# Attention and feed-forward on one core: outputs turned by DMA, loads on GpSimd, first values kept on chip, scores one block further ahead

## The chip, the core and the metric

The kernel runs on one core of a Trainium2 chip. The core has TensorE (PE in the profile, its weight loads PEld), VectorE (DVE), ScalarE (ACT), GpSimd (POOL) and SyncE (SP), each with its own instruction queue that runs in order, and 16 DMA engines that they share. The metric is the device time of one launch in microseconds (us); the median of several runs is compared.

## The reference

Two stages. Block-sparse attention over 4 batches, 8 heads, 768 positions, head size 64, in blocks of 32 positions (24 blocks): a query block sees its neighbours, the first and the last block, and three sampled blocks; the first and the last query block see everything. Then, on the 3072 tokens of 512 numbers, a bilinear feed-forward network (FFN) with 1536 hidden units.

```python
scores = (q @ k.T) / sqrt(64)
mask = |block_q - block_k| <= 1, or either is block 0 or 23, or block_k in sampled_blocks[block_q]
attn = softmax(where(mask, scores, -1e9))
x = (attn @ v), heads side by side          # 3072 x 512
out = ((x @ w_a) * (x @ w_b)) @ w_out       # 512 -> 1536 -> 512
```

## The kernel before

**Units and chunks.** A unit is one batch and one query block, 96 in all; 22 of each 24 are sparse (gathered keys and values), two are dense. Eight units make a chunk (256 tokens); there are twelve chunks, and the second chunk of the first batch is done first. For a unit, TensorE makes the scores of all eight heads (two quads of four heads, each head in 32 of 128 rows), VectorE finds the maximum, ScalarE takes the exponential, the weights are turned so that keys lie on partitions, and TensorE multiplies them with the values. The first batch works in float32 and turns with TensorE (`plain_turn`, L1039); the others split each float32 into two float16 halves (`in_parts`, L951 to L958) and turn by a DMA transpose on SyncE (L1135 sparse, L1239 dense).

**Gathers.** Each sparse unit needs its eight key blocks side by side (`gather_keys`, copies on GpSimd, L653 to L662) and its eight value blocks (`gather_after`, DMAs on SyncE, L714 to L719). Three block numbers are only known at run time: both gathers read them from a small table into registers first (L623, a TENSOR_LOAD). Both gathers have two buffers.

**Output of a pair of units.** `output` divides the sums by the denominators into `xs` (L1292, or L1294 to L1296), lets TensorE transpose it in two float32 matmuls into the sums' own PSUM bank (L1301), and writes the two float16 halves `xT` on ScalarE and VectorE (L1312, L1313).

**FFN.** For a chunk, 12 steps of 24 matmuls (L1350) give the two products of 128 hidden units each, which are multiplied into `g` (L1365, L1368). When all 12 are there, a scale is found, `g` is split (L1402, L1403), and 12 steps of six matmuls (L1432 to L1434) make the output, which ScalarE reads and stores (L1448, L1450). These matmuls fill TensorE between the units of later chunks.

**Weights.** The FFN's weights arrive as 36 tiles of 64-bit numbers (L842, DMAs issued by ScalarE) during the first batch; VectorE and ScalarE convert each tile (L865 to L871, L887 to L895).

**Order.** A planner in the kernel simulates the engines with a cost for each step and writes every engine's instructions out in the order that it finds; each engine then runs its list in order. `LAG` is one of its rules: from unit 24 on, a unit's scores come after the values of the unit three before it. DMAs of SyncE and ScalarE share eight semaphores in turn, so that each waits for the one eight before it to land.

## Time and profile before

| | |
|---|---|
| three runs | 824.20, 828.27, 829.44 us; median 828.27 |
| the profiled execution | 832.1 us, its span 830.3 us |
| TensorE busy | 757.6 us, 91% of the span |
| VectorE, ScalarE, GpSimd busy | 525.1, 485.3, 172.7 us |
| granted TensorE clock, mean | 0.971 of full speed |

The median is 3.8 us below the profiled execution. Busy time is the union of an engine's instructions. Queue instructions (DMA issues, register reads, semaphore waits) do not count as busy; the rows mark them with a q (SPq, ACTq, POOLq).

### The profile page before, as it was taken

The numbers are of one execution on the slowest core, as the hardware profiler recorded it, in microseconds if no ns is written. First come the engines' busy times: TensorE is split into PE (matmuls) and PEld (weight loads), VectorE is DVE, ScalarE is ACT, GpSimd is POOL, SyncE is SP. The second block draws the span as 40 slices with busy tenths as digits, with TensorE's granted clock in tenths as the row PEclk, the third lists the DMA queues.
The fourth block names the chain that finished last, engine by engine and source line by source line (L and its number), as shares of the span: only waits on it lengthen the run. The fifth ranks groups of instructions, "written<-read, shape, count | busy, mean of one in ns | idle before, by whom it ended". The sixth has DMA issues, their size and how long they took to land.

```text
span 830.3 us, 26115 instructions
## 1 busy us (share of the span) xinstructions
PE 757.6 (91%) x10128; PEld 533.0 (64%) x10128; DVE 525.1 (63%) x1495; ACT 485.3 (58%) x1189; POOL 172.7 (21%) x430
## 2 busy tenths in 40 slices
PE   3759699999997989899799999999999999999998
PEld 1426477764586468748558848848758668768853
DVE  3679998866746755686657676766566666532232
ACT  3456777886646554775645666766456655533333
POOL 4405321012123321130223221301123212000000
PEclk9859999999999899999999999999999999999999
DMA  7788877477577688869777779769776665440001
GB/s 226 224 280 252 240 198 213 147 206 176 135 149 144 139 213 148 178 167 185 175 162 137 151 181 228 174 162 188 148 151 148 128 124 128 111 116 2 1 1 52
DMA packets 171803, 130.50 MB, mean 157 GB/s; under 512 B 116894, under 2 KB 138527, under 8 KB 171679
## 3 DMA queue, kind: packets, MB, share of 16 engines
q1 hardware_dynamic: 156844, 86.29, 48.6%
q10 hardware_dynamic: 14832, 42.54, 17.0%
q8 instruction: 80, 1.31, 0.7%
q14 instruction: 47, 0.36, 0.1%
HBM read 86.31 MB, written 11.01 MB: 117 GB/s over the span
## 4 chain that ended last, share of the span: by engine, by line
PE 72%; DMA 10%; DVE 8%; ACT 5%; SPq 2%; issue 2%; ACTq 0%; POOL 0%; POOLq 0%; DVEq 0%
PE ab L1350 40%; PE o L1432 6%; PE o L1434 6%; PE o L1433 6%; PE av L991 5%; PE s L932 4%; DMA VG<-in_v_dram 3%; DMA keysT<-ks 2%; PE av L1301 2%; PE s L923 2%; DMA VG<-vd 2%; ACT gh L1402 1%; DVE gh L1403 1%; PE tp L1039 1%; DMA QZ<-in_q_dram 1%
## 5 line engine op out<-in xcount | busy, mean ns | idle before, releaser
L1350 PE MATMUL ab<-xT,wab 128*128 128x256 f16 x3456 | 396.0, 274 | 2.7 <-DVE g L1368 2.7
L1350 PEld LDWEIGHTS <-wab 128*128 128x128 f16 x3456 | 334.1, 98 | 58.1 <-issue 17.1
L1368 DVE TENSOR_TENSOR g<-g,ab 128x256 f32<-128x256 f32 x144 | 60.4, 419 | 145.8 <-ACT g L1365 141.9
L1365 ACT ACTIVATE g<-ab,f 128x256 f32<-128x256 f32 x144 | 67.9, 471 | 110.5 <-PE ab L1350 106.8
L1402 ACT ACTIVATE gh<-g,scale 128x256 f16<-128x256 f32 x144 | 70.5, 504 | 79.4 <-PE o L1434 74.0
L1403 DVE SCALAR_TENSOR_TENSOR gh<-g,scale,gh 128x256 f16<-128x256 f32 x144 | 68.8, 490 | 75.1 <-ACT gh L1402 73.9
L1432 PE MATMUL o<-wo,gh 128*128 128x512 f16 x288 | 110.4, 383 | 0.1
L1434 PE MATMUL o<-wo,gh 128*128 128x512 f16 x288 | 110.2, 383 | 0.0
L1433 PE MATMUL o<-wo,gh 128*128 128x512 f16 x288 | 110.2, 383 | 0.0
L653 POOL COPY KG<-keysT 128x384 int32<-128x384 int32 (+1 forms) x86 | 47.8, 556 | 278.8 <-PE s L932 237.8
L662 POOL COPY KG<-keysT 128x128 int32 (+1 forms) x264 | 92.6, 388 | 51.8 <-POOL KG L653 32.3
L1095 ACT ACTIVATE sm<-s,low,cq 128x256 f32<-128x256 f32 x132 | 73.7, 560 | 47.4 <-DVE low L1089 38.8
L991 PE MATMUL av<-VG,pt 128*32 128x128 f16 (+2 forms) x3584 | 68.4, 217 | 27.2 <-DMA VG<-in_v_dram 13.0
L421 POOL PARTITION_ALL_REDUCE power<-bound x58 | 22.7, 391 | 296.0 <-DVE bound L1382 126.9
L958 DVE SCALAR_TENSOR_TENSOR hl<-sm,hl 128x256 f16<-128x256 f32 (+1 forms) x156 | 69.6, 450 | 1.7
L1083 DVE TENSOR_REDUCE low<-s 128x2 f32<-128x512 f32 x88 | 60.2, 684 | 13.9 <-PE s L923 9.0
L991 PEld LDWEIGHTS <-pt 128*32 128x32 f16 x2688 | 33.0, 97 | 34.8 <-issue 22.5
L1434 PEld LDWEIGHTS <-gh 128*128 128x128 f16 x288 | 28.4, 99 | 34.6 <-issue 0.8
L1432 PEld LDWEIGHTS <-gh 128*128 128x128 f16 x288 | 28.2, 98 | 34.8 <-issue 4.3
L1433 PEld LDWEIGHTS <-gh 128*128 128x128 f16 x288 | 28.3, 98 | 28.6 <-issue 0.6
L1372 ACT ACTIVATE junk<-g 128x1024 f16<-128x1024 f32 x36 | 38.0, 1055 | 8.5 <-DVE g L1368 8.5
L954 DVE TENSOR_SCALAR hl<-sm 128x256 f16<-128x256 f32 (+1 forms) x125 | 39.3, 317 | 5.5 <-ACT sm L1095 5.2
(122 smaller groups left out, 876.0 us busy)
## 6 DMA issues: line engine op xcount, KB each, us to landing
VG<-vd SPq DMA_DIRECT2D x210, 64.0 KB, 2.2
VG<-vd SPq DMA_DIRECT2D x66, 192.0 KB, 3.2
VG<-vd SPq DMA_DIRECT2D x24, 384.0 KB, 3.8
out_dram<-ou ACTq DMA_DIRECT2D x24, 256.0 KB, 3.5
VG<-in_v_dram SPq DMA_DIRECT2D x74, 64.0 KB, 3.7
stage<-in_v_dram ACTq DMA_DIRECT2D x12, 384.0 KB, 6.7
q<-in_q_dram ACTq DMA_DIRECT2D x18, 256.0 KB, 4.6
vd<-vs SPq DMA_DIRECT2D x12, 384.0 KB, 4.2
```

The source lines that it names most:

```text
L662: nc.gpsimd.tensor_copy(to[:, :, (5 + r) * w : (6 + r) * w], of[:, :, bass.ds(at, w)])
L958: t = yield dve(221 + n * 1.03, lambda: nc.vector.scalar_tensor_tensor(lo, sm, over, hi, ALU.mult, ALU.subtract))
L991: mm(both[hs, :, i % 2, hq] if two else av[hs, i % 2, hq], pt[:, y, hs], of if two or b == 0 else of[:, 0], start=(i % 2 == 0 and hq == 0 ...
L1095: t = yield act(750, lambda hq=hq: nc.scalar.activation(sm[:, hq], ps[:, hq], AF.Exp, bias=low[:, at, hq, 0:1], scale=factor_of(b, cc, hq) ...
L1350: mm(ab[:, i, :], wab[:, f, i, part, kt, :], xc[:, kt, a, :], start=(i == 0 and kt == 0 and part + a == 0), stop=(kt == KT - 1 and a == 1) ...
L1365: yield act(460, lambda: nc.scalar.activation(g, ab[:, 0, :], AF.Copy, scale=f1[:, f : f + 1]))
L1368: t = yield dve(415, lambda: nc.vector.tensor_mul(g, g, ab[:, 1, :]))
L1402: yield act(400, lambda: nc.scalar.activation(gh[:, 0], g, AF.Copy, scale=s))
L1403: t = yield dve(480, lambda: nc.vector.scalar_tensor_tensor(gh[:, 1], g, s, gh[:, 0], ALU.mult, ALU.subtract))
L1432: mm(po, gh[:, 0, js], wo[:, f, 0], start=(f == 0), stop=False)
L1433: mm(po, gh[:, 0, js], wo[:, f, 1], start=False, stop=False)
L1434: mm(po, gh[:, 1, js], wo[:, f, 0], start=False, stop=(f == NF - 1))
```

## The change

Ten edits in one:

- `output`, batches 1 to 3: `xs` is split into two float16 halves `xo` (ScalarE, VectorE), one DMA transpose on SyncE writes them into `xT`, and the PSUM bank is given back once the sums are read. TensorE's transposes stay in batch 0 alone. The layout of `xT` changes for it: `[P, 4, 2, 2, KT, 32]` in place of `[P, KT, 2, 256]`, so an FFN matmul reads its 256 columns in eight runs of 32.
- All loads but those of the first batch's keys, queries, values and the tables, and the stores of the output, are issued by GpSimd instead of ScalarE (`pool_load`).
- SyncE reads the block numbers of up to four units with one TENSOR_LOAD (`starts_of`).
- The host lays the queries out twice (both partition halves), each load is twice as large, and the DMAs that copied one half to the other (`turn_queries`) are gone.
- The first batch's values are loaded once into three tiles in the buffers of `g` (`plain_values_in`). The first eight units (`NEAR`) take their three neighbouring blocks from there by copies on VectorE or ScalarE (`near_values`), and the dense unit (0, 0) reads them in place. Before, the values were loaded for their maximum into a part of the weights' tiles, which held back half of the weights (`parked`), and every gather read the DRAM.
- `LAG` is 4 instead of 3. `KS_BUFS` is 2 instead of 3; `xo` has two buffers.
- The planner's costs know GpSimd's DMAs, so all engines' lists are written anew.

```diff
-KS_BUFS = 3
+KS_BUFS = 2
+XO_BUFS = 2
+LATE_XO = 1000
+LATE_XT = 2500
...
+AT_ONCE = 4
+NEAR = 8
+LATE_X = 800
+LATE_X0 = 0
...
-LAG = 3
+LAG = 4
...
+
+
+def pool_load(moved, fn):
+
+    return [Way("POOL", 1000, fn, moved, 1000)]
...
     VG = [kvp.tile([P, 2, ROW], F16, name=f"VG{i}") for i in range(VG_BUFS)]
-    xT = [kvp.tile([P, KT, 2, CH], F16, name=f"xT{i}") for i in range(X_BUFS)]
+    xT = [kvp.tile([P, PER // 2, 2, 2, KT, BLK], F16, name=f"xT{i}") for i in range(X_BUFS)]
     plain_keys = keysT[0].rearrange("p h s -> p (h s)").bitcast(F32).rearrange(
...
     )
+    resident, resident_held = [], []
     plain_values = v[0].rearrange("g p x -> (g p x)").rearrange("(s x) -> s x", x=H * D)
...
-        yield load_way(1000, lambda: nc.scalar.dma_start(raw, k[b, g]))
+        yield pool_load(1000, lambda: nc.gpsimd.dma_start(raw, k[b, g]))
...
         k_ready[b].fire(end)
+    def plain_block(j):
+
+        t, at = divmod(j, P // BLK)
+        return resident[t // 2][at * BLK : (at + 1) * BLK, t % 2]
+
+    def plain_values_in(r):
+
+        resident_held.append((yield from take("g", G_BUFS)))
+        tt = work.tile([P, 2, H * D], F32, tag="g", name=f"vp{r}", bufs=G_BUFS)
+        resident.append(tt)
+        t = yield load_way(1300, lambda: nc.scalar.dma_start(
+            tt, plain_values.rearrange("(t p) x -> p t x", p=P)[:, 2 * r : 2 * r + 2]
+        ))
+        v_here.fire(t)
+        if r + 1 < NT // 2:
+            plan.start(plain_values_in(r + 1), R_V)
+        else:
+            plan.start(values(1, 0), order[1, 0] - LEAD_V)
+        done = yield from take("ks", KS_BUFS)
+        spare = work.tile([P, 2, H * D], F16, tag="ks", name=f"va{r}", bufs=KS_BUFS)
+        end = yield act(1060, lambda: nc.scalar.activation(
+            spare, tt, AF.Abs, accum_out=bound_v[:, r : r + 1]
+        ))
+        done.fire(end)
+        v_bound[0].fire(end)
+        if r == NT // 2 - 1:
+            plan.start(values_scale(0), order[0, 0] - LEAD_V)
+
     def values(b, g):
...
         raw, freed = yield from raw_tile(b, g, 1)
-        yield load_way(1000, lambda: nc.scalar.dma_start(raw, v[b, g]))
+        yield pool_load(1000, lambda: nc.gpsimd.dma_start(raw, v[b, g]))
         if g + 1 < NG:
-            plan.start(values(b, g + 1), order[b, 0] - LEAD_V if b else R_V)
-        elif b == 0:
-            plan.start(values(1, 0), order[1, 0] - LEAD_V)
+            plan.start(values(b, g + 1), order[b, 0] - LEAD_V)
         elif b + 1 < B:
...
         t = raw.rearrange("p (t x) -> p t x", t=NT)
-        done = yield from take("ks", KS_BUFS)
-        spare = work.tile([P, 2 * NT, P], F16, tag="ks", name=f"va{b}_{g}", bufs=KS_BUFS)
         end = yield act(1020, lambda: nc.scalar.activation(
-            spare[:, :NT], t, AF.Abs,
-            accum_out=bound_v[:, b * NG + g : b * NG + g + 1],
-        ))
-        done.fire(end)
+            junk.rearrange("p f c -> p (f c)")[:, : NT * P].rearrange("p (t x) -> p t x", t=NT),
+            t, AF.Abs, accum_out=bound_v[:, b * NG + g : b * NG + g + 1],
+        ))
         v_bound[b].fire(end)
...
             plan.start(values_scale(b), order[b, 0] - LEAD_V)
-        if b == 0:
-            freed.fire(end)
-            return
         yield v_scale[b]
...
         )[1]
+    def starts_of(b, i):
+
+        if (b, i) not in starts_kept:
+            c = i // PER
+            last = min(i + AT_ONCE, (c + 1) * PER, NB - 1)
+            got = nc.values_load_multi_w_load_instructions(
+                offs[0:1, i:last, :NR].rearrange("p a b -> p (a b)"),
+                engines=(mybir.EngineType.SP,), min_val=0, max_val=S - BLK,
+                skip_runtime_bounds_check_because="the table is clamped to these bounds",
+            )[1]
+            for x in range(i, last):
+                starts_kept[b, x] = got[(x - i) * NR : (x - i + 1) * NR]
+        return starts_kept.pop((b, i))
+
+    starts_kept = {}
     kg_holds, vg_holds = {}, {}
...
             yield from gather_after(n)
+    def near_values(b, i, to):
+        yield v_here
+
+        def copies(eng):
+            def fn():
+                for x in range(3):
+                    eng(to[x * BLK : (x + 1) * BLK, 0, :], plain_block(i - 1 + x))
+            return fn
+
+        t = yield [
+            Way("ACT", 1740, copies(nc.scalar.copy)),
+            Way("DVE", 1000, copies(nc.vector.tensor_copy)),
+        ]
+        vg_ready[b, i, 0].fire(t)
+
     def gather_after(n):
...
                 return
-            nc.sync.dma_start(to[0 : 3 * BLK, 0, :], of[(i - 1) * BLK : (i + 2) * BLK, :])
+            if not near:
+                nc.sync.dma_start(to[0 : 3 * BLK, 0, :], of[(i - 1) * BLK : (i + 2) * BLK, :])
             if first:
...
                 nc.sync.dma_start(to[0:BLK, 1, :], of[(NB - 1) * BLK :, :])
-            for r, at in enumerate(dynamic("SP", offs, i)):
+            for r, at in enumerate(starts_of(b, i)):
                 nc.sync.dma_start(
...
                 )
-        t = yield [Way("SP", 475 if dense else 2300 + 800 * first, copies, 1300, 1)]
+        near = order[b, i] < NEAR
+        if near:
+            plan.start(near_values(b, i, to), order[b, i] - LEAD_G)
+        t = yield [Way("SP", 475 if dense else 2300 - 700 * ((b, i) in starts_kept) - 400 * near + 800 * first, copies, 800 if near else 1300, 1)]
         vg_ready[b, i, x].fire(t + LATE_VG)
...
             t = work.tile([P, NG, CH], F32, tag="rq", name=f"q{cc}_{half}", bufs=1)
-            end = yield load_way(700, lambda t=t, half=half: nc.scalar.dma_start(
-                t[:D], q[b, c, :, half * NG : (half + 1) * NG]
+            end = yield pool_load(2000, lambda t=t, half=half: nc.gpsimd.dma_start(
+                t, q[b, c, :, half * NG : (half + 1) * NG]
             ))
...
         heads = slice(half * NG, (half + 1) * NG)
-        high, low_ = QT[cc][:D, 0, heads], QT[cc][:D, 1, heads]
+        high, low_ = QT[cc][:, 0, heads], QT[cc][:, 1, heads]
         yield act(1230, lambda: nc.scalar.activation(
-            high, t[:D], AF.Abs, accum_out=bound[:D, at : at + 1]
+            high, t, AF.Abs, accum_out=bound[:, at : at + 1]
         ))
...
         known.fire(end)
-        s = scale[:D, at : at + 1]
-        end = yield act(1120, lambda: nc.scalar.activation(high, t[:D], AF.Copy, scale=s))
-        plan.start(turn_queries(cc, half, 0), u0 - LEAD_Q, end)
+        s = scale[:, at : at + 1]
+        yield act(1120, lambda: nc.scalar.activation(high, t, AF.Copy, scale=s))
         end = yield dve(1250, lambda: nc.vector.scalar_tensor_tensor(
-            low_, t[:D], s, high, ALU.mult, ALU.subtract
+            low_, t, s, high, ALU.mult, ALU.subtract
         ))
         freed.fire(end)
-        plan.start(turn_queries(cc, half, 1), u0 - LEAD_Q, end)
+        q_ready[cc].fire(end)
     def next_queries(cc):
...
         )[half].bitcast(I32)[:, at * 2 * DM : (at + 1) * 2 * DM]
-        end = yield load_way(1350, lambda: nc.scalar.dma_start(
+        end = yield pool_load(1350, lambda: nc.gpsimd.dma_start(
             raw, (w_a, w_b, w_out)[i][f].bitcast(I32)
...
             yield act(470, lambda: nc.scalar.copy(xs, sums[:, 1]))
-            yield dve(418, lambda: nc.vector.tensor_add(xs, xs, sums[:, 0]))
+            t = yield dve(418, lambda: nc.vector.tensor_add(xs, xs, sums[:, 0]))
+            read.fire(t + LATE_AV)
             yield dve(430, lambda: nc.vector.tensor_mul(xs, xs, over))
-        ps = bank[:, 1].rearrange("p (g i x) -> p g i x", g=NG, i=2)
+            gone = yield from take("xo", XO_BUFS)
+            xo = work.tile([P, 2, 2, P], F16, tag="xo", name=f"xo{b}_{i}", bufs=XO_BUFS)
+            flat = xs.rearrange("p i a d -> p i (a d)")
+            yield act(400, lambda: nc.scalar.copy(xo[:, 0], flat))
+            t = yield dve(420, lambda: nc.vector.tensor_sub(xo[:, 1], flat, xo[:, 0]))
+            held.fire(t)
+            t = yield sp(900, 760, lambda: nc.sync.dma_start_transpose(
+                to.rearrange("p a x k q -> p (a x) (k q)"), xo.rearrange("p a i c -> p (a i c)")
+            ))
+            gone.fire(t + LATE_XO)
+            x_ready[cc].fire(t + LATE_XT)
+            x_ready[cc].fire(t + LATE_XT)
+            return
+        ps = bank[:, 1].rearrange("p (i c) -> p i c", i=2)
+        yield LATE_X if b else LATE_X0
         def turns_():
...
                 nc.tensor.transpose(
-                    ps[:, :, x], xs[:, x].rearrange("p a d -> p (a d)"), eye
+                    ps[:, x], xs[:, x].rearrange("p a d -> p (a d)"), eye
                 )
...
                                 mm(
-                                    ab[:, i, :], wab[:, f, i, part, kt, :], xc[:, kt, a, :],
+                                    ab[:, i, :].rearrange("p (j x q) -> p j x q", j=PER // 2, x=2),
+                                    wab[:, f, i, part, kt, :], xc[:, :, a, :, kt, :],
                                     start=(i == 0 and kt == 0 and part + a == 0),
...
-        t = yield load_way(728, lambda: nc.scalar.dma_start(rows, o))
+        t = yield pool_load(728, lambda: nc.gpsimd.dma_start(rows, o))
...
+        a = np.concatenate([a, a], axis=2)
```

Three places in the lists, before and now. First SyncE, in the third batch, between two units: `pt` is a unit's turned weights, `VG` the gathered values, `vd` the values in DRAM, `xo` and `xT` the output's halves before and after the turn. Before:

```order
L1135 DMA_TRANSPOSE pt_7845<-hl_7732 128x8x128
L714 DMA VG_85<-vd_80 96x1024
L623 TENSOR_LOAD offs
L719 ISA
L719 DMA VG_85<-vd_80 32x1024
```

and now:

```order
L1187 DMA_TRANSPOSE pt_7764<-hl_7685 128x8x128
L1368 DMA_TRANSPOSE xT_86<-xo_2_7836 128x4x128
L778 DMA VG_85<-vd_80 96x1024
L783 ISA
L783 DMA VG_85<-vd_80 32x1024
```

The register read is gone from most gathers (24 are left of 88), and every second unit a transpose of the outputs stands ahead of a gather.

Second TensorE, second batch, in the second products (`o`) of a chunk, between the steps of two hidden tiles `gh`. Before:

```order
L1434 LDWEIGHTS gh_0_4557
L1434 MATMUL o_1_4589<-wo,gh_0_4557 128x512
L1301 MATMUL av_6_4329<-eye,xs_6_4553 128x4x32 x2
L1432 LDWEIGHTS gh_1_4558
L1432 MATMUL o_0_4588<-wo,gh_1_4558 128x512
```

and now:

```order
L1514 LDWEIGHTS gh_0_4947
L1514 MATMUL o_1_4986<-wo,gh_0_4947 128x512
L1512 LDWEIGHTS gh_1_4948
L1512 MATMUL o_0_4985<-wo,gh_1_4948 128x512
L1513 LDWEIGHTS gh_1_4948
```

The pair of transposes between them is gone; of 48 such pairs in the list 12 are left, all in batch 0.

Third GpSimd, first batch, between the key gathers (`KG`) of two units. Before:

```order
L662 COPY KG_83<-keysT_76 128x4x32
L653 COPY KG_82<-keysT_76 128x4x96
L623 TENSOR_LOAD offs
L662 ISA
L662 COPY KG_82<-keysT_76 128x4x32
```

and now:

```order
L710 COPY KG_83<-keysT_76 128x4x32
L898 DMA stage<-in_moe_w_out_dram 128x1024
L701 COPY KG_82<-keysT_76 128x4x96
L656 TENSOR_LOAD offs
L710 ISA
L710 COPY KG_82<-keysT_76 128x4x32
```

A weight load now stands between two gathers on the same queue; the first two of the 36 stand ahead of the first gather.

## Rows read from the trace of the kernel before

**Rows 1.** The page: TensorE busy, and the granted clock, in 40 slices (tenths).

```profile
PE   3759699999997989899799999999999999999998
PEclk9859999999999899999999999999999999999999
```

**Rows 2.** Stretches: from:to, us, then each engine's busy us, clock, DMA share, GB/s.

```profile
0.00:60.00 60.00, 32.57 (x489) 17.29 (x489) 33.13 (x106) 29.24 (x80) 19.59 (x49) 0.82 0.79 237
60.00:140.00 80.00, 68.79 (x1036) 50.43 (x1037) 75.83 (x193) 57.05 (x153) 28.47 (x58) 0.92 0.77 228
220.00:760.00 540.00, 514.42 (x7347) 370.95 (x7346) 339.18 (x996) 311.79 (x771) 114.00 (x297) 0.99 0.72 154
260.00:280.00 20.00, 13.95 (x257) 8.20 (x248) 13.57 (x46) 14.00 (x35) 6.27 (x19) 0.83 0.75 146
300.00:320.00 20.00, 17.09 (x226) 13.97 (x225) 11.26 (x37) 11.30 (x26) 3.69 (x11) 0.91 0.82 193
400.00:420.00 20.00, 15.69 (x225) 7.88 (x222) 12.87 (x39) 10.76 (x26) 5.40 (x13) 0.91 0.67 156
```

**Rows 3.** Waits of TensorE, 0 to 60 us: us in total, times, longest.

```profile
PE s L1068 <- DVE mrows L497: 7.4, 1, 7.4
PE av L991 <- DMA VG<-in_v_dram: 6.6, 2, 3.9
PE s L923 <- DMA wab<-in_v_dram: 5.0, 1, 5.0
```

**Rows 4.** Waits of TensorE, 200 to 760 us.

```profile
PE av L1301 <- DVE xs L1296: 8.5, 8, 1.5
PE av L991 <- DMA VG<-vd: 5.9, 5, 2.9
PE av L991 <- DMA pt<-hl: 4.5, 1, 4.5
PE av L1301 <- ACT gh L1402: 4.5, 2, 4.2
```

**Rows 5.** Groups of TensorE by form, 220 to 830 us: busy, mean ns, idle before.

```profile
L991 PE MATMUL av<-VG,pt 128*32 128x128 f16 x1332 | 43.3, 224 | 10.5 <-DMA VG<-vd 5.9 <-DMA pt<-hl 4.5
L991 PE MATMUL av<-VG,pt 128*32 128x64 f16 x1332 | 40.0, 194 | 0.0
L1301 PE MATMUL av<-eye,xs 128*128 128x128 f32 x72 | 14.8, 287 | 13.7 <-DVE xs L1296 8.5 <-ACT gh L1402 4.5 <-DVE low L1089 0.4
```

**Rows 6.** Timeline of TensorE around 264 us: start, us, line, [idle before].

```profile
260.81 2.79 PE L1350 MATMUL ab<-xT,wab 128*128 128x256 f16 x24
...
264.51 0.43 PE L1301 MATMUL av<-eye,xs 128*128 128x128 f32 x2
269.45 0.83 PE L991 MATMUL av<-VG,pt 128*32 128x128 f16 x32 [4.51 <-DMA pt<-hl]
```

**Rows 7.** SyncE's queue by line: ns min/median/max, first to last start.

```profile
L1135 SPq DMA_TRANSPOSE pt<-hl x66: 1231/1274/2644, 231.2 to 716.6; - x66
L623 SPq TENSOR_LOAD <-offs x88: 662/684/1623, 13.7 to 714.3; - x88
L822 SPq DMA_DIRECT2D QT<-QT x36: 467/546/1271, 165.9 to 654.3; - x36
```

**Rows 8.** The page's DMA issues: KB each, median us to landing.

```profile
out_dram<-ou ACTq DMA_DIRECT2D x24, 256.0 KB, 3.5
pt<-hl SPq DMA_TRANSPOSE x90, 3.6
```

**Rows 9.** Groups by form, whole span, of the output's two halves.

```profile
L1312 ACT ACTIVATE xT<-av 128x256 f16<-128x256 f32 x36 | 13.5, 375 | 3.9 <-PE av L1301 3.9
L1313 DVE SCALAR_TENSOR_TENSOR xT<-av,xT 128x256 f16<-128x256 f32 x36 | 15.0, 418 | 1.9 <-ACT xT L1312 1.8
```

**Rows 10.** GpSimd's and ScalarE's queues by line: ns min/median/max, first to last start.

```profile
L623 POOLq TENSOR_LOAD <-offs x22: 724/728/955, 3.0 to 131.5; - x22
L842 ACTq DMA_DIRECT2D keysT<-in_moe_w_a_dram x8: 329/334/357, 31.5 to 145.7; - x8
```

More of the change, by code (lines that the diff above doesn't have):

```diff
@@ L182, in begin @@
         if way.moved:
-            at = max(at, self.dma - way.ahead, self.generator)
+            at = max(at, self.dma - way.ahead, self.generator if way.eng != "POOL" else 0.0)
             if len(self.landed) >= LANES:
@@ L193, in issue @@
             turn = way.eng == "SP" and way.ns != 650 and not way.extra
-            self.generator = at + (625 if turn else way.ns if way.extra else 455)
-            start = max(self.dma, at + (1275 if turn else 1100 if way.eng == "SP" else 1241))
+            if way.eng != "POOL":
+                self.generator = at + (625 if turn else way.ns if way.extra else 455)
+            begun = 1275 if turn else {"SP": 1100, "ACT": 1241, "POOL": 1900}[way.eng]
+            start = max(self.dma, at + begun)
             self.dma = start + way.moved
@@ L296 @@
     B, NCH, D, H, CH = q.shape
+    D //= 2
     NF, P, DM = w_a.shape
@@ L381 @@
     k_free = [Event(NB) for _ in range(B)]
-    v_bound = [Event(NG) for _ in range(B)]
+    v_bound = [Event(NG if b else NT // 2) for b in range(B)]
+    v_here = Event(NT // 2)
     v_scale = [Event() for _ in range(B)]
     v_stored = [Event(NG) for _ in range(B)]
-    q_ready = [Event(3 if cc < NCH else 5) for cc in range(NC)]
+    q_ready = [Event(3) for _ in range(NC)]
     tables = Event()
@@ L398 @@
         dense = i in (0, NB - 1)
+        if (b, i) == (0, 0):
+            continue
         vg_units += [(b, i, x) for x in range(2 * HQ if dense else 1)]
     vg_order = {u: m for m, u in enumerate(vg_units)}
-    vg_ready = {u: Event() for u in vg_units}
+    vg_ready = {u: Event(2 if order[u[:2]] < NEAR else 1) for u in vg_units}
     s_sent = {u: Event() for u in units}
@@ L508, in raw_tile @@
     def raw_tile(b, g, n):
-        if b == 0:
-            late = wab[:, NF // 2 :].rearrange("p f i a c x -> p (f i a c x)").bitcast(F32)
-            late = late.rearrange("p (g x) -> p g x", x=2 * NT * D)
-            return late[:, g], parked
         yield stage_freed
@@ L612, in values_scale @@
         yield dve(150, lambda: nc.vector.reduce_max(
-            bound[:, at : at + 1], bound_v[:, b * NG : (b + 1) * NG],
+            bound[:, at : at + 1], bound_v[:, b * NG : b * NG + (NG if b else NT // 2)],
             axis=mybir.AxisListType.X,
@@ L816, in plain_queries @@
         next_queries(cc)
-    def turn_queries(cc, half, a):
-        heads = slice(half * NG, (half + 1) * NG)
-        yield SPARE
-        end = yield sp(650, 400, lambda: nc.sync.dma_start(
-            QT[cc][D:, 1 - a, heads], QT[cc][:D, a, heads]
-        ))
-        q_ready[cc].fire(end)
     def weights(n):
@@ L1245, in all_values @@
     def all_values(b, i, hq, x, pt, kept):
-        m = vg_order[b, i, 2 * hq + x]
-        yield vg_ready[b, i, 2 * hq + x]
+        if (b, i) == (0, 0):
+            yield v_here
+        else:
+            m = vg_order[b, i, 2 * hq + x]
+            yield vg_ready[b, i, 2 * hq + x]
         if hq == 0 and x == 0:
@@ L1251, in all_values @@
             yield all_done[b, i, 2 * hq + x - 1]
-        if b == 0:
+        if (b, i) == (0, 0):
+            terms = [
+                (pt, (y,), resident[(3 * x + y) // 2][:, (3 * x + y) % 2, 4 * D * hq : 4 * D * (hq + 1)])
+                for y in range(3)
+            ]
+        elif b == 0:
             vg = plain_vg(m).rearrange("p a x -> p (a x)")
@@ L1261, in all_values @@
         kept.fire(t)
-        vg_free[m].fire(t)
+        if (b, i) != (0, 0):
+            vg_free[m].fire(t)
+        elif (hq, x) == (HQ - 1, 1):
+            for held in resident_held:
+                held.fire(t)
         all_done[b, i, 2 * hq + x].fire(t)
@@ L1309, in output @@
         s = scale[:, at_v : at_v + 1] if b == 0 else 1.0
-        of = ps.rearrange("p g i x -> p g (i x)")
-        hi, lo = to[:, :, 0], to[:, :, 1]
+        of = ps.rearrange("p i c -> p (i c)")
+        hi, lo = (to[:, a].rearrange("p x k q -> p (x k q)") for a in range(2))
         yield act(470, lambda: nc.scalar.activation(hi, of, AF.Copy, scale=s))
@@ L1461 @@
         plan.start(make_tables(), -40)
-        plan.start(values(0, 0), R_V)
+        plan.start(plain_values_in(0), R_V)
         plan.start(weights(0), R_L)
```

11 lines of the change are left out of this document (3 added, 8 removed).

## The prediction

> **What bounds the kernel now.** I read the page's slices first, then the busy times by stretch, then TensorE's waits, then the groups of the lines that the change touches. The slices [rows 1] show two regimes. In the first quarter TensorE's digits wander between 3 and 9 and its granted clock dips to 5, a slice in which it stood at its lower level, 1.2 of 2.4 GHz, for most of the time; from a quarter on they are 9 or close to it, with a few dents. The stretches [rows 2] put numbers to it. From 220 to 760 us TensorE is busy 514.4 of 540 us: its work is the bound there, and what leaves its list leaves the time. From 60 to 140 us VectorE is the fuller one, 75.8 of 80 us against TensorE's 68.8, while the weights are converted. Before 60 us nothing is full (TensorE 32.6, VectorE 33.1 of 60): the time goes by latencies, and the waits say which [rows 3]: 7.4 us for the mask at the start, 6.6 us for the gathered values of two units, 5.0 us for the first loads. After 200 us TensorE's waits are of two sorts [rows 4]: for `xs` ahead of its transposes (8.5 us; another 4.5 us ahead of the same transposes is put down to ScalarE's `gh`), and for a unit's gathered values or turned weights (5.9 and 4.5 us).
>
> **The change, part by part.** The sum is made against the profiled execution, 832.1 us.
>
> *Transposes of the output.* In batches 1 to 3, 72 of them go, 14.8 us of TensorE's busy time [rows 5]. They lie in the stretch where TensorE is the bound: 14.8 us gained.
>
> *The wait before them.* The same row shows 13.7 us of idle TensorE ahead of those matmuls. As TensorE runs its list in order, everything behind stood still for a result that only the next chunk needs. Now the list goes on; some of what comes next will not be ready either. Bounds 0 and 13.7; I take 11, nearer the upper end, since FFN matmuls mostly come next.
>
> *What replaces them.* ScalarE and VectorE lose 375 and 418 ns for each of 36 pairs and gain a copy and a subtraction of the same size [rows 9], so nothing. SyncE gains 36 transposes; an issue of the twice as large one takes 1.27 us [rows 7], so at most 46 us in 540. It loses three quarters of the register reads, 64 of 88 at 0.68 us, 44 us, and 36 copies of queries at 0.55 us, 20 us [rows 7]. Behind a transpose that waits for `xo` stand the next unit's value gathers. They have the fourth block of lead to hide in. `xT` is ready later than before by some 4 us: a landing takes 3.6 us behind the issue's start [rows 8], plus queueing, in place of a 0.43 us pair of transposes. If the cover of other matmuls is gone that delays the first product of a chunk, nine chunks in all: bounds 0 and 9 x 4 = 36 us. In the list at least three FFN steps of 2.8 us [rows 6], or as much of the second products, stand between a chunk's last values and its first product, so I take 6 us, nearer 0.
>
> *The fourth block and the single register read.* The 66 sparse transposes are issued over 485 us [rows 7], one unit in 7.4 us. One block more of lead gives a unit's softmax, turn and gather that much more time before TensorE wants them. The worst wait, 4.5 us for turned weights [rows 6], is shorter than that. What is late next is a gather whose buffer is still read, since there are only two. Of 10.4 us [rows 4] I take 7, bounds 0 and 10.4. After such waits the clock was at its lower level for a part of the stretch: granted 0.83, 0.91 and 0.91 of three stretches of 20 us [rows 2], which is 20 x (0.17 + 0.09 + 0.09) = 7.0 us lost. I take 4 of them, bounds 0 and 7.
>
> *Batch 0.* The first eight units no longer fetch their neighbours from DRAM. Two waits for gathered values fall there, 6.6 us [rows 3]; their three sampled blocks are still fetched, so 3 to 4 us of it may go. Weights start earlier: in the list the first two loads stand ahead of the first key gather, and conversions can fill some of VectorE's 27 idle us before 60 us, which relieves the stretch where VectorE is full. The near blocks cost VectorE or ScalarE three copies of 512 columns a unit, each at most twice the 0.42 us of a 256-column operation [rows 9]: 20 us in all, in the part with room. Against it, those two loads, 1.05 MB, share the DMA engines with the keys that the first scores wait for: at 237 GB/s [rows 2] 4.4 us at most. Bounds: a loss of 5 (nothing gained, keys late) and a gain of 20 (the waits, and most of VectorE's early idle time turned to use, 13 us of 27). I take a gain of 8, between the two and nearer the lower, because TensorE has no other work before 60 us.
>
> *Loads on GpSimd, queries twice.* ScalarE is spared some hundred issues at 0.33 us [rows 10]; it is not the bound. An issue on GpSimd is not in this trace. Nearest rows: 0.33 us on ScalarE, 0.73 us for GpSimd's own register read [rows 10], 1.27 us for the dearest issue [rows 7]. At 1 us, 36 weight loads in 140 us are hidden: GpSimd is busy 48.1 us there [rows 2] and reads registers for 22 x 0.73 = 16 us [rows 10]. If the cover is gone the price is in the rival below. The doubled queries are asked for nine units, 67 us, ahead. The last store is issued by GpSimd: its 3.5 us to landing [rows 8] is the tail, and 1 us more is taken, bounds 0 and 3.
>
> Sum: 14.8 + 11 + 7 + 4 + 8 - 6 - 1 = 37.8 us, so 794.3 us for a profiled execution. The median of the runs lies 3.8 us under the profiled one: **790 us**.
>
> **The rivals.**
>
> *GpSimd sets the pace of batch 0 (slower).* Each unit's key gather now stands behind weight loads on one in-order queue. Of the first 140 us 140 - 48.1 - 16 = 76 us are free, 2.1 us for each of the 36 loads. From that price on GpSimd paces the batch, and each further us costs 36. The 38 us are eaten at 3.2 us, and from 3.4 us on the kernel is slower by 8. At 3.5 us it would take 790 + 36 x 1.4 = 840 us. For it: VectorE is 95% busy from 60 to 140 us [rows 2], and GpSimd's queue has no second path. Against it: no issue row is above 1.3 us in the median [rows 7, 10]. 6%. The Trainium skill (SBUF — State Buffer, section "SBUF: two separate sides") says that a DMA issued from GpSimd has its descriptors written by that engine, which is locked out while VectorE runs certain copies; its example goes from about 620 to 3100 ns. By that rule, as an estimate, an issue would come to about the price at which the gain is gone. No run here shows it.
>
> *The outputs come late.* If SyncE's queue holds the transposes back, nine chunks wait 2 to 4 us more than taken: 804 to 818 us, say 808. For: the eight waits for `xs` show that this chain is late at times [rows 4]. Against: three FFN steps of 2.8 us [rows 6] in between. 13%.
>
> *Batch 0 gains nothing.* VectorE, full from 60 to 140 us [rows 2], has the same conversions and the near copies on top: 790 + 8 = 798, to 803 with the keys late. 17%.
>
> *All waits go.* Waits and clock at their upper bounds: 2.7 + 3.4 + 3 more, and 7 more from late outputs and the tail, 774 us; with batch 0 at its best 762. 15%.
>
> *Matmuls pay for short runs.* An FFN matmul's columns now come in eight runs of 32. At 5 cycles a run at 2.4 GHz, 3456 of them would lose 8 x 5 / 2.4 = 17 ns each, 58 us: 848. Against: value matmuls of 128 columns in two runs take 224 ns, those of 64 in one run 194 [rows 5], 30 ns more where 64 columns alone are 27. 3%.
>
> That the change does not do what it says is nearly excluded: in the lists 36 of 48 pairs of transposes and 64 of 88 reads are gone.
>
> **How the numbers follow.** The forecast's own cases, 780 to 798, have 43%; the rivals 54%; 3% is left for a near draw by several mishaps. The likeliest is 790. The range goes from 770 (half of the best case is left out below) to 813 (late outputs, batch 0 without gain): about 2 in 10 stay outside. A difference of 1%, 8 us, is what runs that scatter by 5 us can tell from none. Faster by more than that (below 820) holds in the forecast, the best case, batch 0 without gain and nearly all of the late outputs: 0.87. Within 1%: 0.04 (the near draw and the end of the late outputs). Slower: 0.09 (GpSimd's pace, short runs).
>
> **What would show it.** Right: no transposes of `xs` after the first batch; TensorE's busy time near 743 us, its idle time after 220 us below 15 us, no dent of the clock there; GpSimd's issues near 1 us. Wrong: waits of the FFN's first products for `xT`; scores that wait for GpSimd's gathers in the first 140 us; an FFN step of 24 matmuls above 2.8 us; first scores later than before by more than 5 us.

## The result, and the profile after

The changed kernel takes 808.23 us (median of 5 runs, 803.08 to 809.06) against 828.93 us for the kernel before on the same chip: a ratio of 0.9745, 95% interval 0.9712 to 0.9777. That is 20.7 us faster. Medians here and below are of all runs of a kernel, while the ratios are taken from its runs in the faster of the two states that an execution can fall in. The forecast was 790 us, within 770 to 813. The sign and the range held; the gain was a little over half of the 38 us forecast. The profiled execution took 803.08 us with a span of 801.3 us.

The page's slices of the changed kernel, TensorE and its granted clock, stand against [rows 1]:

```profile
PE   2759789899998989999999999999989999999997
PEclk9879999999999999999999999999999999999999
```

From a quarter of the span on, TensorE's dents are nearly gone. Its stretches (from:to, us, busy us of each engine, clock, DMA share, GB/s) answer to [rows 2]:

```profile
0.00:60.00 60.00, 31.28 (x470) 16.30 (x470) 47.15 (x136) 30.73 (x82) 29.29 (x65) 0.86 0.79 240
60.00:140.00 80.00, 71.13 (x1108) 52.20 (x1109) 78.39 (x199) 64.94 (x171) 42.23 (x82) 0.95 0.73 215
220.00:760.00 540.00, 528.61 (x7421) 386.81 (x7414) 336.13 (x980) 321.05 (x789) 133.86 (x333) 1.00 0.74 159
260.00:280.00 20.00, 19.47 (x335) 14.99 (x334) 14.07 (x46) 12.48 (x33) 9.31 (x22) 1.00 0.83 176
300.00:320.00 20.00, 20.00 (x312) 17.06 (x310) 14.93 (x46) 15.60 (x38) 6.49 (x16) 1.00 1.03 232
400.00:420.00 20.00, 19.83 (x257) 11.75 (x255) 14.74 (x43) 12.88 (x36) 6.82 (x18) 1.00 0.70 174
580.00:600.00 20.00, 17.80 (x247) 11.59 (x247) 11.70 (x38) 12.60 (x32) 6.59 (x16) 0.91 0.87 181
```

The three stretches whose clock was 0.83 and 0.91 are at 1.00; one new dent of 0.91 stands at 580 us. Before 60 us TensorE does no more than before (31.3 against 32.6 us), while VectorE went from 33.1 to 47.2 us. TensorE's waits after 200 us, against [rows 4]:

```profile
PE av L1043 <- DMA VG<-vd: 9.4, 8, 2.4
PE s L984 <- ACT sm L1260: 1.0, 2, 0.8
PE av L1043 <- DMA pt<-hl: 0.5, 1, 0.5
```

No wait for `xs` is left, the wait for turned weights fell from 4.5 to 0.5 us, and the one for gathered values grew from 5.9 to 9.4 us. Its waits in the first 60 us, against [rows 3]:

```profile
PE s L1120 <- DVE mrows L516: 8.3, 1, 8.3
PE tp L1091 <- ACT sm L1147: 5.9, 5, 1.8
PE s L975 <- POOL KG L710: 4.9, 1, 4.9
PE av L1380 <- DVE xs L1356: 3.3, 2, 3.1
PE av L1043 <- ACT pt L1096: 1.6, 1, 1.6
```

The 6.6 us for gathered values are gone, and others stand in their place. The groups of TensorE from 220 to 830 us, against [rows 5, 6]: an FFN matmul takes 273 ns, as it did (24 of them 2.79 us), and no group of transposes is left.

```profile
L1429 PE MATMUL ab<-xT,wab 128*128 128x256 f16 x2856 | 322.7, 273 | 0.0
L1043 PE MATMUL av<-VG,pt 128*32 128x128 f16 x1296 | 42.3, 223 | 10.1 <-DMA VG<-vd 9.4 <-DMA pt<-hl 0.5
```

SyncE's queue by line from 220 to 760 us, against [rows 7] (ns min/median/max, first to last start), the new transposes with their landing, and GpSimd's issues of weights by form from 0 to 160 us (busy us, mean ns), against [rows 10]:

```profile
L1368 SPq DMA_TRANSPOSE xT<-xo x36: 1188/1224/2099, 231.8 to 706.8; - x36
...
DMA to landing us min/median/max: 2.5/2.6/4.6
L666 SPq TENSOR_LOAD <-offs x17: 752/1023/2502, 238.6 to 664.6; - x17
```

```profile
L898 POOL DMA_DIRECT2D keysT<-in_moe_w_a_dram x8 | 4.5, 567 | 15.6 <-DVE w L925 10.1 <-DVE wab L925 5.3 <-DVE power L443 0.2
```

**Where the time came from, in the two profiled executions.** TensorE was busy for 742.4 us in place of 757.6. The gaps between its matmuls, with the time ahead of the first one, came to 42.4 us before 220 us (43.2 in the kernel before) and to 11.4 us behind it (25.6). So the gain is 15.2 us of busy time and 14.2 us of gaps behind 220 us; the gaps before 220 us, where the first batch lies, gave 0.8 us, and the end of the span lost 1.1.

The 15.2 us are not the transposes alone. The pages of four kernels give TensorE's busy time with the number of its matmuls: the kernel before (mean granted clock 0.971), GpSimd's loads alone (experiment 3 below, 0.982), the turn alone (experiment 1, 0.969) and the changed kernel (0.983):

```profile
PE 757.6 (91%) x10128; PEld 533.0 (64%) x10128; DVE 525.1 (63%) x1495; ACT 485.3 (58%) x1189; POOL 172.7 (21%) x430
PE 750.6 (91%) x10128; PEld 530.7 (65%) x10128; DVE 518.3 (63%) x1487; ACT 487.1 (59%) x1197; POOL 222.5 (27%) x518
PE 751.9 (90%) x10056; PEld 526.6 (63%) x10056; DVE 517.4 (62%) x1482; ACT 492.1 (59%) x1202; POOL 166.1 (20%) x430
PE 742.4 (93%) x10056; PEld 522.5 (65%) x10056; DVE 533.6 (67%) x1504; ACT 490.9 (61%) x1202; POOL 227.6 (28%) x532
```

The same number of matmuls takes 7 us (10128) and 9.5 us (10056) less in the kernel with the higher clock. At a like clock, 72 matmuls fewer make 5.7 us (757.6 less 751.9), 8.2 us (750.6 less 742.4) or 12.4 us (754.8 in experiment 2, clock 0.981, less 742.4). So of the 15.2 us some 6 to 12 are the transposes, and the other 3 to 9 go with the higher clock.

### The profile page after: what moved, and what is told of

Same layout as the page of the kernel before. It is cut to its first block, busy times and chain, and to the rows that moved or that the text cites. A ratio compares the mean times of both kernels' runs of the same rounds, so it can differ in the third digit from the quotient of the medians.

```text
span 801.3 us, 25888 instructions
## 1 busy us (share of the span) xinstructions
PE 742.4 (93%) x10056; PEld 522.5 (65%) x10056; DVE 533.6 (67%) x1504; ACT 490.9 (61%) x1202; POOL 227.6 (28%) x532
## 4 chain that ended last, share of the span: by engine, by line
PE 65%; DVE 13%; DMA 9%; issue 5%; ACT 4%; SPq 3%; POOL 0%; POOLq 0%; ACTq 0%; DVEq 0%
PE ab L1429 37%; PE o L1512 6%; PE o L1514 5%; PE o L1513 5%; PE av L1043 5%; PE s L984 4%; DMA VG<-vd 4%; DMA vd<-vs 2%; DMA vp<-in_v_dram 2%; DVE low L1135 1%; SPq L666 1%; DVE wab L947 1%; SPq L783 1%; PE s L1120 1%; PE s L975 1%
## 5 line engine op out<-in xcount | busy, mean ns | idle before, releaser
L710 POOL COPY KG<-keysT 128x128 int32 (+1 forms) x264 | 89.0, 375 | 44.6 <-POOL KG L701 22.5
L701 POOL COPY KG<-keysT 128x384 int32<-128x384 int32 (+1 forms) x86 | 50.6, 589 | 164.6 <-PE s L984 146.0
L1147 ACT ACTIVATE sm<-s,low,cq 128x256 f32<-128x256 f32 x132 | 73.6, 559 | 31.7 <-DVE low L1141 15.6
L440 POOL PARTITION_ALL_REDUCE power<-bound x58 | 25.8, 447 | 180.1 <-DVE bound L1462 103.7
L1043 PE MATMUL av<-VG,pt 128*32 128x128 f16 (+2 forms) x3488 | 63.5, 212 | 13.0 <-DMA VG<-vd 9.4
L1043 PEld LDWEIGHTS <-pt 128*32 128x32 f16 x2688 | 33.1, 97 | 35.4 <-issue 26.6
L1452 ACT ACTIVATE junk<-g 128x1024 f16<-128x1024 f32 x36 | 38.0, 1055 | 10.4 <-DVE g L1448 10.2
L1006 DVE TENSOR_SCALAR hl<-sm 128x256 f16<-128x256 f32 (+1 forms) x113 | 36.3, 325 | 11.7 <-DMA pt<-hl 8.9
```

The source lines that it names most:

```text
L710: nc.gpsimd.tensor_copy(to[:, :, (5 + r) * w : (6 + r) * w], of[:, :, bass.ds(at, w)])
L1043: mm(both[hs, :, i % 2, hq] if two else av[hs, i % 2, hq], pt[:, y, hs], of if two or b == 0 else of[:, 0], start=(i % 2 == 0 and hq == 0 ...
L1147: t = yield act(750, lambda hq=hq: nc.scalar.activation(sm[:, hq], ps[:, hq], AF.Exp, bias=low[:, at, hq, 0:1], scale=factor_of(b, cc, hq) ...
```

## The experiments

My first theory was that the output's turn by DMA carries the gain and that the rest comes out at nothing. All ratios below are to the kernel before on the same chip. The changed kernel was not run again beside the experiments, so a comparison with it is the quotient of two such ratios. "Queue" is the summed duration of what SyncE issues and loads into registers from 220 to 760 us; "gaps" are TensorE's after 220 us. Both are added up from the trace of one execution, whose time is the last column. It lies up to 10 us from the median, so gaps and median need not go together.

| kernel | median us | ratio, 95% interval | queue us | gaps us | profiled us |
|---|---|---|---|---|---|
| before | 828.9 | 1 | 361 | 25.6 | 832.1 |
| changed | 808.2 | 0.9745 (0.9712 to 0.9777) | 351 | 11.4 | 803.1 |
| turn alone | 848.1 | 1.0241 (1.0184 to 1.0299) | 397 | 33.1 | 838.3 |
| turn undone | 820.4 | 0.9880 (0.9843 to 0.9916) | 310 | 15.6 | 821.4 |
| GpSimd's loads alone | 833.2 | 0.9992 (0.9948 to 1.0035) | 344 | 16.4 | 824.1 |
| third block | 818.0 | 0.9847 (0.9796 to 0.9899) | 366 | 23.0 | 821.4 |
| turn + fourth block | 857.1 | 1.0331 (1.0281 to 1.0380) | 422 | 43.4 | 858.4 |
| turn + relief of SyncE | 847.3 | 1.0186 (1.0130 to 1.0242) | 364 | 36.3 | 849.2 |
| one read each | 827.9 | 0.9982 (0.9947 to 1.0018) | 387 | 24.2 | 831.8 |
| ScalarE's loads | 830.1 | 1.0016 (0.9978 to 1.0053) | 355 | 24.4 | 827.1 |
| ScalarE's loads, same order | 813.4 | 0.9784 (0.9747 to 0.9821) | 351 | 16.2 | 813.3 |
| one read each, same order | 827.2 | 0.9930 (0.9896 to 0.9963) | 379 | 26.8 | 824.4 |
| margin 60 ns | 817.3 | 0.9819 (0.9768 to 0.9869) | 358 | 18.6 | 815.2 |
| near copies on GpSimd | 805.8 | 0.9700 (0.9665 to 0.9734) | 353 | 11.0 | 805.3 |

**1. The turn alone, in the kernel before.** Abridged:

```diff
-KS_BUFS = 3
+KS_BUFS = 2
+XO_BUFS = 2
-xT = [P, KT, 2, CH]
+xT = [P, PER // 2, 2, 2, KT, BLK]
 # output(), b > 0, in place of the two transposes on TensorE:
+nc.scalar.copy(xo[:, 0], flat)
+nc.vector.tensor_sub(xo[:, 1], flat, xo[:, 0])
+nc.sync.dma_start_transpose(to, xo)
```

> The kernel before with one part of the change alone: in batches 1 to 3 the output is split in two 16-bit halves and turned by DMA (two conversion buffers instead of three make the room). Theory (the turn carries the gain, the other parts come out at about nothing): the 72 matmuls of 14.8 us and the 13.7 us of waits before them go, so 802 to 811 us, as fast as the whole change. Rival (loads, fetches and the queue's fourth block carry a good part): at most half of the gain, 815 to 822 us. In the profile both want no wait for xs after 220 us.

It took 848 us: 2.4% slower than before by the ratio, 2.1% by the medians on its chip (848.1 against 830.5), outside both expectations. TensorE's waits after 220 us in this kernel:

```profile
PE av L994 <- DMA pt<-hl: 9.8, 8, 2.6
PE ab L1367 <- DVE g L1386: 8.5, 6, 4.9
PE av L994 <- DMA VG<-vd: 7.2, 5, 3.2
PE o L1450 <- ACT gh L1420: 6.2, 4, 3.9
```

The `xs` waits are gone as forecast, and more came in their place: turned weights and gathered values together 17.0 us against 10.4 [rows 4]. Both start on SyncE's queue, which now carries 36 transposes more. But the FFN's own waits, for `g` and `gh`, grew further: 14.7 us against 1.4 for `g` before (the 4.5 us for `gh` [rows 4] then stood ahead of the transposes). Those end on VectorE and ScalarE, so SyncE's queue is not shown to be the whole of the loss. Besides, this is the fastest of the six runs, 10 us under their median; its span is 6 us longer than in the trace of the kernel before, and what the slower runs lost is not seen. My first theory fell here.

**2. The turn undone, in the changed kernel.** In `output()` the branch of the diff above is taken out, and TensorE transposes in every batch.

> The changed kernel with the output turned by TensorE again in batches 1 to 3, everything else kept. Theory: it loses what the turn gave, 824 to 833 us, level with the kernel before within 4 us. Rival: the other parts carry some of the gain, 814 to 822 us. The units' longer lead (four blocks) could cover the waits before the 72 matmuls in either: then some of the 13.7 us stay away and 816 to 820 us come out by the 14.8 us of matmuls alone.

820 us, 1.4% above the changed kernel (quotient of the ratios 1.014, give or take 0.005). So the turn gives some 11 us here, close to the difference in TensorE's busy time (754.8 against 742.4 us), and the third expectation is the one that came. The order is a new one, though, and experiment 11 shows what that alone can do. After 220 us the waits ahead of the transposes are two rows:

```profile
PE av L1366 <- DVE xs L1360: 1.1, 4, 0.3
PE av L1366 <- DVE rscale L446: 1.0, 1, 1.0
```

2.1 us in place of 13.7: these waits can leave without the turn.

**3. GpSimd's loads alone, in the kernel before.** Keys, values, weights and the store; the loads of the queries stay on ScalarE. The planner is given its new prices for GpSimd's DMAs, so the order is a new one.

```diff
-yield load_way(1000, lambda: nc.scalar.dma_start(raw, k[b, g]))
+yield pool_load(1000, lambda: nc.gpsimd.dma_start(raw, k[b, g]))
 # and so for v, the weights and the store
```

> The kernel before with GpSimd starting the loads of keys, values, queries' neighbours in the weights, and the store of the output, instead of ScalarE; nothing else (queries still as before). Theory: within 3 us of the kernel before (826 to 832 us), since ScalarE was not what TensorE waited for. Rival (ScalarE freed of the issues lets batch 0 run ahead): 4 to 8 us less.

No difference, as the theory had it. The Trainium skill (DMA: Bandwidth & Descriptors, section "Issuing engines are not separate DMA queues") says that transfers run on the same 16 engines whoever starts them; the ratio of 0.9992 is in line with that, though it does not test it.

**4. Scores wait for the third block again, in the changed kernel.** `LAG = 4` becomes `3`.

> The changed kernel with scores waiting for the third block behind again, not the fourth. Theory: the waits for gathered values (9.9 us in batches 1 to 3) are set by the two buffers of values, not by the lead, so within 3 us of the changed kernel: 805 to 811 us. Rival (the forecast's term of 7 us for the longer lead is in the time): 813 to 817 us, with waits for turned weights back at 4 us or more in the trace.

818 us: the rival's side, 1.0% above the changed kernel (give or take 0.6%), in an order of its own. Its waits for turned weights after 220 us:

```profile
PE av L1043 <- DMA pt<-hl: 11.4, 4, 4.0
```

They were 0.5 us in the changed kernel. The waits for gathered values are 5.9 us here against 9.4, so that the two together rise by 7.4 us.

**5 and 6. The turn with the longer lead, and the turn with SyncE's queue relieved, in the kernel before.** Abridged:

```diff
 # 5: experiment 1, and
-LAG = 3
+LAG = 4
 # 6: experiment 1 (LAG = 3), and
-for r, at in enumerate(dynamic("SP", offs, i)):
+for r, at in enumerate(starts_of(b, i)):      # AT_ONCE = 4
-plan.start(turn_queries(cc, half, 0), u0 - LEAD_Q, end)
+q_ready[cc].fire(end)                         # queries doubled
```

> The kernel before with the output's turn by DMA and, beside it, scores that wait for the fourth block behind. The turn alone took 848 us: the 36 transposes put 48 us more on SyncE's queue (397 us of issues and register loads between 220 and 760 us, before 361) and waits for turned weights and gathered values came in the place of the 13.7 us. Theory A (a full queue needs a longer lead): the fourth block alone takes most of it back, 818 to 828 us. Theory B (a full queue needs fewer entries, lead or not): 838 to 850 us.

> The kernel before with the output's turn by DMA and with SyncE's queue relieved as in the change: twelve numbers read at once (33 us of register loads less between 220 and 760 us) and queries doubled in memory, so that the 36 copies of queries go (17 us of issues there less); scores still wait for the third block, loads still start on ScalarE. Theory B: the queue falls to 345 to 355 us and the time to 815 to 826 us. Theory A: 836 to 848 us, the relief without the lead gives little.

857 and 847 us. Theory A fell by the first and theory B by the second; 847 us lies where A had put the relief, but the lead that A relied on made the kernel slower. Neither part alone makes the turn pay, and the two together were not tried there. In experiment 6 the queue did fall, to 364 us where the kernel before has 361, and the gaps were 36 us all the same: 15.8 us for gathered values and turned weights, and 16.8 us for the FFN's `g` and `gh`. So the length of SyncE's queue does not decide by itself. Each of these kernels also has an order of its own, which the planner made anew, and that was the next question.

**7 and 8. One read of three numbers for each block, and loads on ScalarE, in the changed kernel.** `AT_ONCE = 4` becomes `1`; each `pool_load(...)` becomes a `load_way(...)` on ScalarE.

> The changed kernel with one read of three numbers for each block again, the rest kept: SyncE's queue gets back some 33 us of register loads between 220 and 760 us. Theory A (the lead covers the queue): within 4 us of the changed kernel, 805 to 813 us. Theory B: 815 to 828 us, with waits for turned weights or gathered values of 8 us or more beyond the 9.9 us.

> The changed kernel with keys, values, queries, weights and the store started by ScalarE again. ScalarE gets back 21 us of issues between 220 and 760 us, of 540 us in which it is busy for 321. Theory (ScalarE has room after batch 0, and batch 0 waits for VectorE): within 4 us of the changed kernel, 804 to 813 us. Rival (a load waits behind ScalarE's work, or its work behind the load): 814 us or more, lost between 20 and 220 us.

828 and 830 us: either edit takes the whole gain away. For the loads that agrees badly with experiment 3.

**9 and 10. The same two edits with the order kept.** The planner is told the old price, and only the instruction handed out differs. Abridged:

```diff
 # 9: Way("POOL", 1000, ...) stays, and
-nc.gpsimd.dma_start(raw, k[b, g])
+nc.scalar.dma_start(raw, k[b, g])
 # 10: starts_kept is filled as before, and
-return starts_kept.pop((b, i))
+starts_kept.pop((b, i)); return dynamic("SP", offs, i)
```

> The changed kernel with the loads and the store started by ScalarE, but planned as if GpSimd started them: TensorE, VectorE and SyncE get the same instructions in the same order as in the changed kernel, ScalarE its own with the 109 issues between them. With a plan of its own the same edit took 830 us. Theory C (the 22 us were the new order, not the issuing engine): 804 to 813 us. Theory D (the issuing engine costs them, by ScalarE held up or by queues that meet): 822 us or more.

> The changed kernel with a read of three numbers for each block, planned as if twelve were read at once: TensorE, VectorE and ScalarE keep their order to the row, SyncE has 64 register loads more, some 33 us between 220 and 760 us. With a plan of its own the same edit took 828 us. Theory C (order): 806 to 813 us. Theory D (SyncE's queue is what it costs): 818 us or more, with values that wait for gathers for 15 us or more after 220 us.

The two part ways: theory C holds for the loads, theory D for the reads. Loads on ScalarE cost 0.4% (1.004 to the changed kernel, give or take 0.005) once the order is kept: nearly all of experiment 8 was the new order. The reads cost 1.9% (give or take 0.5%) with the order kept, and 2.4% in an order of their own. With the order kept only SyncE's queue differs, so it is the queue that costs the 1.9%. In experiment 10 after 220 us:

```profile
PE av L1043 <- DMA VG<-vd: 15.3, 13, 4.3
PE av L1043 <- DMA pt<-hl: 6.9, 7, 1.9
```

22.2 us against 9.9. One such place shows the queue at work. First SyncE in the changed kernel (start us, us, line, count), then SyncE and TensorE in experiment 10, the same instructions of the same units:

```profile
277.35 1.34 SPq L783 DMA_DIRECT2D VG<-vd  x3
278.79 0.36 SPq L778 DMA_DIRECT2D VG<-vd  x1
279.39 2.21 SPq L783 DMA_DIRECT2D VG<-vd  x3
```

```profile
282.01 1.32 SPq L783 DMA_DIRECT2D VG<-vd  x3
283.43 0.36 SPq L778 DMA_DIRECT2D VG<-vd  x1
284.75 3.10 SPq L783 DMA_DIRECT2D VG<-vd  x3
```

```profile
288.39 0.35 PE L1043 MATMUL av<-VG,pt 128*32 128x128 f16 x8 [4.33 <-DMA VG<-vd]
289.77 0.67 PE L1043 MATMUL av<-VG,pt 128*32 128x128 f16 x24 [1.04 <-DMA VG<-vd]
```

Between the last unit's first gather and its sampled ones stand 0.24 us in the changed kernel (279.15 to 279.39) and 0.96 us here, the room of a register load of 0.68 us. The last row is longer too, 3.10 against 2.21 us: within it SyncE waits for something that the profile puts down to the landing of a transpose of weights (us, times, longest, 274 to 290 us):

```profile
SPq L783 <- DMA pt<-hl: 1.8, 1, 1.8
```

TensorE then stands for 4.33 us before those values and for 1.04 us more, where it stood for 2.38 us in the changed kernel. So a part of the loss is the register loads themselves, and a part what a later queue runs into.

**11. A margin of 60 ns in place of 50.** `M_ACT = 50` becomes `60`: the planner adds 10 ns more ahead of ScalarE's steps. All work stays.

> The changed kernel with one constant of the planner changed, the 50 ns that it adds before a ScalarE instruction after 45 us made 60 ns: every engine does the same work, in another order. Theory C (the time hangs on the order by some 2%): 812 to 828 us. Theory D (the order does little, the parts do it): 804 to 812 us.

817 us, 0.8% above the changed kernel (give or take 0.6%). An order made by another hair costs about as much as the fourth block (experiment 4). It is one other order; how the time spreads over many was not tried, so that a part of the changed kernel's gain may be a lucky order. By experiments 8 and 9 an order can cost 2.4%.

**12. Near copies on GpSimd, order kept.**

```diff
-Way("DVE", 1000, copies(nc.vector.tensor_copy)),
+Way("DVE", 1000, copies(nc.gpsimd.tensor_copy)),
```

> The changed kernel with the copies of the first values that VectorE makes (21 of 443 ns, 9.3 us between 25 and 52 us) made by GpSimd, order and all else kept. Theory (VectorE sets batch 0's pace): waits for xs of 15.6 us fall to 8 to 11 us and the time by 3 to 6 us, 802 to 806 us. Rival (the xs waits come from the chain, not from VectorE's load): within 2 us of the changed kernel. Another: GpSimd is slower at them, and values wait for them: 2 to 6 us more.

805.8 us. The ratio, 0.9700, is the lowest of all, but it is 0.5% below the changed kernel's, give or take 0.5%, so this version is not told apart from it. VectorE lost 6.5 us of work before 60 us, the values waited 3.8 us for GpSimd's copies, and the waits for `xs` stayed at 16.5 us against 15.6:

```profile
0.00:60.00 60.00, 30.03 (x470) 15.76 (x470) 40.67 (x115) 30.24 (x81) 43.17 (x86) 0.88 0.80 242
```

```profile
PE av L1380 <- DVE xs L1356: 16.5, 8, 4.6
```

So they do not hang on the near copies. The longest in the changed kernel, TensorE and then VectorE (start us, us, line), points to the place of `xs` in VectorE's list:

```profile
54.90 0.65 PE L1043 MATMUL av<-VG,pt 128*32 128x64 f32 x32
60.71 0.69 PE L1380 MATMUL av<-eye,xs 128*128 128x128 f32 x2 [5.16 <-DVE xs L1356]
```

```profile
55.06 1.41 DVE L947 SCALAR_TENSOR_TENSOR wab<-wab,scale 128x512 f16<-128x512 f32 x2
56.38 0.55 DVE L1245 TENSOR_REDUCE low<-s 128x1 f32<-128x384 f32 x1
56.92 0.74 DVE L947 SCALAR_TENSOR_TENSOR wo<-wo,scale 128x512 f16<-128x512 f32 x1
...
59.63 0.69 DVE L922 SCALAR_TENSOR_TENSOR wab<-keysT,wab 128x512 int32<-128x512 int32 x1
60.23 0.42 DVE L1356 TENSOR_TENSOR xs<-av,den 128x256 f32<-128x256 f32 x1
```

The values end at 55.55 us; weight conversions and other units' steps stand ahead of `xs` without a pause until 60.23 us. That an earlier place would help was not tried.

## Why the prediction was right, and where it was not

Measured on the profiled executions (832.1 to 803.1 us, 29.0 where 37.8 were forecast), step by step.

- **Transposes of the output, 14.8 us: right that they go, too large as a price.** The 14.8 us count every matmul to its end, where it overlaps with its neighbours. One pair in the kernel before:

```profile
297.31 0.71 PE L1350 MATMUL ab<-xT,wab 128*128 128x256 f16 x5
297.85 0.38 PE L1301 MATMUL av<-eye,xs 128*128 128x128 f32 x2
298.07 0.60 PE L1350 MATMUL ab<-xT,wab 128*128 128x256 f16 x4
```

The pair's own time is 0.38 us, but from its start to the start of what follows pass 0.22 us. For all 36 pairs that adds up to 10.2 us, within the 6 to 12 us that the busy times above give. That TensorE's busy time came out at 742.4 us ("near 743") is partly luck: a higher clock made up the rest.

- **The wait before them, 11 of 13.7 us: gone whole, for a cause that is only half as I put it.** Experiment 2 keeps the transposes and still has only 2.1 us of it. So something else in the change can free TensorE of these waits too, the longer lead or the new order; the two were not separated.
- **What replaces them on SyncE, "nothing": this is the step that I undervalued.** I set 46 us of new issues against 64 us relieved and left it at that. The runs show that the queue matters: without the single read alone the changed kernel loses 1.9% in the same order (experiment 10), and the turn alone makes the kernel before slower (experiment 1). That the balance is the whole condition is not shown, since with the queue relieved the turn still lost there (experiment 6).
- **The fourth block and the single read, 7 of 10.4 us: mis-sized.** The waits for values and turned weights went from 10.4 to 9.9 us only. That the transposes' issues ate what the two parts gave is likely, not shown. Taken away the parts cost far more than 7 us: 15 us for the reads, 8 us for the lead (the latter with an order of its own).
- **Clock, 4 us: about right.** The three dents are gone and one of 0.91 is new, by the forecast's own reckoning 5.2 of 7.0 us; the busy times above leave 3 to 9 us for the clock of the whole execution.
- **Batch 0, 8 us: did not come.** Its gaps fell by 0.8 us. This is the rival "Batch 0 gains nothing", and the largest part of the miss. The waits for values went (13.0 us in the first 220 us), and `xs` (7.1 to 15.6 us) and the first batch's softmax (3.4 to 7.4 us) took their place. Of the rival's reason, the near copies on top of VectorE's work do not explain it: experiment 12 takes them off VectorE and the waits stay, though 3.8 us of new waits came with it. The other steps that stand ahead of `xs` on VectorE, weight conversions among them, are the likely cause.
- **`xT` late, a loss of 6 us: did not come.** No FFN matmul waits for it; a landing takes 2.6 us where 3.6 were taken. The rival "The outputs come late" falls with it.
- **Store, 1 us: right.** From the last matmul to the end of the span 5.2 us pass, 4.0 before; with the store issued by ScalarE in the same order (experiment 9) it is 4.0 again.

These differences add up: 7.2 for batch 0, 6.5 for the waits of values, 3.6 for transposes and clock together (15.2 of 18.8 us), less 2.7 and 6.0 us, is 8.6 of the 8.8 us missing. The other 9 us of the miss lie outside the mechanism: I took the median 3.8 us under the profiled execution, as it was before, and the changed kernel's profiled execution happened to be its fastest, 5.1 us under its median.

**GpSimd sets the pace: refuted.** Its issues take 0.53 to 0.63 us in the mean of each form, where 2.1 us was the point from which it decides. The Trainium skill (SBUF — State Buffer, section "SBUF: two separate sides") speaks of a DMA started by GpSimd that takes about 620 ns alone and 3100 beside a copy on VectorE. No run here shows that: the longest issue of a weight load took 0.76 us, and 0.66 us in the stretch where VectorE was busy for 78.4 of 80 us; the five issues that fell beside its float32 copies of 0.42 us took 0.53 to 0.59 us and landed after 4.0 to 5.6 us. One sign of this rival did show: the first scores wait 4.9 us for a gather of GpSimd. But that gather had itself waited 8.8 us for the load of its keys, and the first scores start 0.9 us later than before (13.56 against 12.68 us). **Short runs: refuted**, 273 ns before and after. The 5 cycles a run that priced this rival were a supposition, and no row stood behind them.

Left open: why the turn loses in the kernel before even with the lead or with the relief, and whether the two together would make it pay. Its order there (experiments 1, 5, 6) is one that the planner made anew; how much of the 2 to 3% is order and how much the queue was not separated, nor were the two conversion buffers, on their own, tried in the kernel before. In the changed kernel the turn and the fourth block were taken out with new orders only, so their 11 and 8 us hold an unknown share of order.

## What to carry to other kernels

Book a new step on the queue that issues it, and ask what else the change takes off that queue: here 64 register loads more on a queue that also carries 36 new transposes cost 15 of the 20.7 us gained. Where a planner sets the order, undo a part with the order kept, and time one harmless change of a constant first: 10 ns moved this kernel by 0.8%, and one edit cost 2.8% with a plan of its own and 0.4% in the old order, so that an ablation with a plan of its own says little below 2 to 3%. Price a matmul by the time from its start to the start of the next, and compare busy times at a like clock. Forecast a ratio of medians; one profiled execution lay up to 10 us from its kernel's.

## What the runs showed of the hardware

- A read of nine or twelve numbers into registers takes SyncE 0.75 to 2.51 us, 1.02 us in the median of 24; one of three 0.68 us.
- Starting a load of 256 to 512 KB costs GpSimd 0.53 to 0.63 us; ScalarE's issue was 0.33 us [rows 10].
- A copy of 32 x 512 in 32 bits takes 418 ns on VectorE, 617 ns on ScalarE and 608 ns on GpSimd (medians).
- A matmul whose 256 columns come in eight runs of 32 takes as long as one with a single run, 273 ns.
- The same 10056 matmuls keep TensorE busy for 742.4 us at a mean granted clock of 0.983 and for 751.9 us at 0.969.
